# Attention and expert layer on one core: squarer transposes, scores two steps ahead, routing work on GpSimd

## The chip, the cores and the metric

The kernel runs on one core of a Trainium2 chip. The metric is the device time of one execution in microseconds. In the core, TensorE (PE in the profile) multiplies, VectorE (DVE), ScalarE (ACT) and GpSimd (POOL) do the rest, and SyncE (SP) issues transfers. Each engine works through its own instructions in the order in which they were written, and waits for the others by semaphores.

## The reference

Local and global causal attention over 4 batches, 8 heads, 768 positions and 64 columns a head, with a slope per head, and then a layer of 8 experts, of which each of the 3072 tokens takes two:

```python
keep = is_global | is_local             # 8 global positions; 96 local ones, the own included
scores = scale * q @ k.T + bias
scores = np.where(keep, scores, -1e9)
a = np.exp(scores - scores.max(-1))
a = a / (a.sum(-1) + 1e-09)
x = (a @ v)                             # then as [3072 tokens, 512]
noisy = x @ w_gate + np.log1p(np.exp(x @ w_noise)) * noise
top2 = two largest of noisy;  top2_w = softmax over the two
for e in range(8):                      # a token's rows for its two experts
    out[mask] += top2_w * (np.maximum(x[mask] @ w1[e], 0) @ w2[e])
```

## The kernel before

**Attention** goes over 24 blocks of 128 tokens (`g`), six to a batch, and in each over four pairs of heads (`hp`). One pass of the loop at the end of the attention part, an iteration, takes two pairs, `n` and `n + 1`; there are 48, and iteration k has n = 2k. A window is 168 keys wide: 96 earlier ones, 8 global ones, and 64 of the block's own, for each half of the 128 tokens. A batch's first block has only the 128 own ones.

- `score(n)` (L606): eight matmuls in the four corners of the array (64 x 64), into two banks of tag `sc`. VectorE adds the bias and takes the maximum (L628), ScalarE the exponential (L632). A pair's two windows lie in one of four standing buffers `a`, with 64 columns of zeros beside each; GpSimd writes the zeros once, at the start (L544).
- `trans(n)` (L635): four transposes a pair, 128 x 128 (L644), two in a first block, and ScalarE's copy (L646).
- `attend(n)` (L650): a pair's eight matmuls with the values (L666), each of 64 output rows; two of them, side by side in the two halves of the columns, run together. VectorE divides (L672 to L675).
- `gate_t`, `gate_l`, `gate_s` (L280 to L299): a block's gate and noise logits.

The order in an iteration is `trans(n)`, `trans(n+1)`, `score(n+2)`, `attend(n-2)`, `attend(n-1)`, and then what the table `todo` holds for these n (filled by `at`): loads, the gate, the splits of weights, the first tiles.

**Routing** is done in five segments of blocks (`SEG`, `route(r)`, L304): softplus as a polynomial in 13 steps (L321 to L336), the two largest (L342, L344), a token's place in its expert's list, and two marks and two entries a block (L408, L409), which TensorE multiplies into the lists (L417). `route` is a generator. `tick()` runs one step of each active segment, eight times an iteration; segments 0 and 1 take every other call. A step stands on VectorE in its place between the scores' reductions. Of a block's two marks one is on GpSimd and one on VectorE.

**Experts.** Each weight is split in two halves of 16 bits, by a scale from its maximum (`scales`, L143: four reductions of 1.2 us, L149). For expert 0 the first weight is split on GpSimd (`split`, L205, L206). After segment 2 (`CLOSE`), expert 0's first four tiles are gathered (L222), scaled and split (`ready`, `rest`, L233 to L250) and transposed (`turn_pe`, L264). Then the experts run: `up(e, c, f)` (L857) and `down`, and in between the rest of segments 3 and 4, the first of them in ten and then up to sixty calls around `up(0, 0, 0)` and `up(0, 0, 1)`. The first three `up` of expert 0 leave their subtraction to GpSimd (L865).

## Time and profile before

| | |
|---|---|
| median of 3 runs | 759.24 us (759.09 to 759.91) |
| the profiled execution | 757.7 us, of which the span 755.9 |
| TensorE busy in the span | 726.4 us, 96% |
| VectorE, ScalarE, GpSimd busy | 487.0, 359.3, 209.7 us |
| granted clock of TensorE, mean | 0.988 |
| iteration 0 of attention starts | 6.90 us |
| the first expert's first matmul | 192.38 us |

A busy share says which engine may be the bound of a stretch; it has to be read stage by stage, since attention and experts have different ones. A row of a timeline gives start, duration, engine, line and operation, output and inputs, shapes, and how many instructions it merges; in square brackets stands the idle time before it with what ended it. A matmul of 32 bits leaves two records. Matmuls overlap, so their spacing is read from the starts of rows.

### The profile page before, as it was taken

What the parts mean: (1) busy time and instruction counts of PE and PEld (TensorE: products, weight loads), DVE (VectorE), ACT (ScalarE), POOL (GpSimd) and SP (SyncE); (2) the same over time, 40 slices, a digit from 0 to 9 for tenths busy, and PEclk for the clock granted to TensorE, in tenths of its full rate; (3) what the DMA queues carried; (4) which work ended last, traced back from release to release, by engine and by line L of the source; (5) the groups of instructions that cost most, each with busy time, mean ns of one, the idle gap of its engine ahead of it and who ended that gap; (6) DMA issues with size and microseconds to landing.
All of it is one profiled execution on the core that took longest, in us unless ns stands there. A gap on an engine that the chain in (4) does not pass through costs nothing.

```text
span 755.9 us, 16638 instructions
## 1 busy us (share of the span) xinstructions
PE 726.4 (96%) x6279; PEld 454.3 (60%) x6279; DVE 487.0 (64%) x1655; ACT 359.3 (48%) x744; POOL 209.7 (28%) x209
## 2 busy tenths in 40 slices
PE   6999999897998999999999999999999999999996
PEld 4878867676544756464656556564656556564762
DVE  5657898878796747673865577276648646763500
ACT  5888787676344424333452434254344424342501
POOL 2000076230237451215031321403140322212014
PEclk9999999998899999999999999999999999999998
DMA  7889688964408865695479459546954864552015
GB/s 217 262 267 281 193 259 274 285 203 160 154 14 161 228 126 170 106 180 104 123 139 141 115 149 171 105 150 107 169 103 144 152 122 129 87 78 33 2 17 77
DMA packets 107673, 112.59 MB, mean 149 GB/s; under 512 B 53216, under 2 KB 66224, under 8 KB 107584
## 3 DMA queue, kind: packets, MB, share of 16 engines
q1 hardware_dynamic: 95104, 84.25, 41.0%
q0 software_dynamic: 11936, 26.92, 20.7%
q8 instruction: 52, 0.85, 0.5%
q14 instruction: 37, 0.30, 0.1%
q10 hardware_dynamic: 544, 0.26, 0.1%
HBM read 71.61 MB, written 28.10 MB: 132 GB/s over the span
## 4 chain that ended last, share of the span: by engine, by line
PE 72%; issue 12%; DVE 9%; POOL 3%; ACT 3%; DMA 1%; POOLq 0%; ACTq 0%; DVEq 0%
PE av L890 16%; PE at L857 15%; PE sc L857 14%; PE av L900 10%; PE at L644 5%; PE av L666 5%; PE sc L621 4%; POOL out_dram L875 2%; DVE ns L628 1%; PE sc L285 1%; DVE entry L409 1%; PE sc L293 1%; PE lg L299 1%; ACT a L632 1%; DVE l L238 1%
## 5 line engine op out<-in xcount | busy, mean ns | idle before, releaser
L875 POOL DMA_INDIRECT out_dram<-y,ids x56 | 88.6, 1583 | 211.7 <-ACT y L874 207.2
L857 PEld LDWEIGHTS <-w1h 128*128 128x128 f16 x1024 | 100.2, 99 | 70.7 <-issue 2.5
L857 PE MATMUL at<-xx,w1h 128*128 128x300 f16 (+1 forms) x512 | 128.7, 339 | 2.1 <-ACT xx L266 1.9
L857 PE MATMUL sc<-xx,w1h 128*128 128x300 f16 (+1 forms) x512 | 126.6, 336 | 0.0
L222 POOL DMA_INDIRECT xg<-xd,ids x56 | 57.4, 1026 | 166.5 <-DVE hl L868 124.2
L890 PE MATMUL av<-w2h,hh 128*128 128x512 f16 x256 | 97.1, 379 | 0.0
L890 PE MATMUL av<-w2l,hh 128*128 128x512 f16 x256 | 97.0, 379 | 0.0
L890 PE MATMUL av<-w2h,hl 128*128 128x512 f16 x256 | 97.0, 379 | 0.0
L857 PE MATMUL at<-xx,w1l 128*128 128x512 f16 (+1 forms) x256 | 86.7, 339 | 0.0
L857 PE MATMUL sc<-xx,w1l 128*128 128x512 f16 (+1 forms) x256 | 85.8, 335 | 0.0
L632 ACT ACTIVATE a<-ns,mx 128x168 f32<-128x168 f32 (+1 forms) x192 | 69.7, 421 | 32.7 <-DVE mx L628 28.4
L890 PEld LDWEIGHTS <-hh 128*128 128x128 f16 x512 | 49.5, 98 | 56.0
L868 DVE SCALAR_TENSOR_TENSOR hl<-sc,hh 128x300 f16<-128x300 f32 (+1 forms) x63 | 36.3, 577 | 67.4 <-ACT hh L867 67.4
L149 DVE TENSOR_REDUCE wmx<-raw 128x1 f32<-128x1024 f32 x64 | 76.5, 1207 | 0.0
L867 ACT ACTIVATE hh<-at 128x300 f16<-128x300 f32 (+1 forms) x62 | 31.2, 502 | 92.8 <-PE at L857 92.8
L900 PE MATMUL av<-hh,w2h 128*128 128x300 f16 x256 | 74.6, 291 | 0.0
L900 PE MATMUL av<-hh,w2l 128*128 128x300 f16 x256 | 74.3, 290 | 0.0
L900 PE MATMUL av<-hl,w2h 128*128 128x300 f16 x256 | 74.1, 290 | 0.0
L628 DVE CUSTOM_DVE_ANT_0 ns<-sc,bias 128x168 f32<-128x168 f32 (+1 forms) x192 | 53.8, 319 | 30.8 <-PE sc L621 19.7
L857 PEld LDWEIGHTS <-w1l 128*128 128x128 f16 x512 | 50.5, 99 | 38.4 <-issue 0.8
L868 DVE SCALAR_TENSOR_TENSOR hl<-at,hh 128x300 f16<-128x300 f32 (+1 forms) x62 | 35.5, 573 | 54.9 <-ACT hh L867 54.9
L242 ACT ACTIVATE xp<-xg,up 128x512 f16<-128x512 f32 x48 | 34.5, 719 | 71.6 <-DVE up L240 63.7
(174 smaller groups left out, 1215.1 us busy)
## 6 DMA issues: line engine op xcount, KB each, us to landing
raw<-in_w SPq DMA_DIRECT2D x32, 1024.0 KB, 7.8
out_dram<-zero SPq DMA_DIRECT2D x14, 512.0 KB, 6.9
vs<-in_v SPq DMA_DIRECT2D x24, 260.0 KB, 3.9
xd<-xr SPq DMA_DIRECT2D x24, 256.0 KB, 2.7
qs<-in_q SPq DMA_DIRECT2D x23, 256.0 KB, 5.9
ks<-in_k SPq DMA_DIRECT2D x19, 272.0 KB, 4.4
vp<-in_v SPq DMA_DIRECT2D x20, 195.0 KB, 5.3
ks<-in_k SPq DMA_DIRECT2D x4, 464.0 KB
```

What stands on the lines that cost most here:

```text
L149: nc.vector.tensor_reduce(m[:, i:i + 1], t[:, i % 2 * n:(i % 2 + 1) * n], op=OP.max, axis=AX.X, apply_absolute_value=True)
L222: nc.gpsimd.indirect_dma_start(out=xg[e, t], out_offset=None, in_=xd[:n], in_offset=bass.IndirectOffsetOnAxis(ap=rows(e, t), axis=0), boun ...
L242: nc.scalar.activation(y[:m, :Dm], x[:, :Dm], AF.Copy, scale=u)
L628: nc.vector.tensor_tensor_reduce(out=ns[:, s, :w], in0=ps[:, s], in1=bias[:, hp, s] if i else bias0[:, hp, s], scale=-scale, scalar=3e38, ...
L632: nc.scalar.activation(A[m][:, s, c:c + w], ns[:, s, :w], AF.Exp, bias=mx[:, s:s + 1], scale=-1.0)
L644: nc.tensor.transpose(p4[:, :, c, s * Q:(s + 1) * Q], x[:, s, a:a + P], ident)
L666: nc.tensor.matmul(ps[y * Q:(y + 1) * Q, h % 4], x[:kk, a:a + Q], t[:kk, c], start=kk < P or not i, stop=kk == P, tile_position=(0, y * Q))
L857: nc.tensor.matmul(ps, w[e % 2][:, k, fs], xx[c][:, x + k, :hh[c].shape[2]], start=n == 0, stop=n == 3 * KC - 1)
L868: nc.vector.scalar_tensor_tensor(hl[c][:, f], ps, 0.0, hh[c][:, f], op0=OP.max, op1=OP.subtract)
L875: ins = nc.gpsimd.indirect_dma_start(out=out, out_offset=bass.IndirectOffsetOnAxis(ap=rows(e, t), axis=0), in_=y, in_offset=None, bounds_c ...
L890: nc.tensor.matmul(ps, x[0][:, f, cols], w[e % 2][:, f], start=n == 0, stop=n == 3 * FC - 1)
L900: nc.tensor.matmul(ps, w[e % 2][:, f, cols], x[1][:, f], start=n == 0, stop=n == 3 * FC - 1)
```

## The change

- Standing buffers `a` go; a pair's two windows lie beside each other in 336 columns, in one of six rotating buffers. `trans` takes three squares of them, at columns 0, 208 and 104 (two squares in a first block), and ScalarE copies 384 columns instead of 512.
- `attend(n)` takes both pairs at once: 16 matmuls as before. Eight use the first two squares, on the two halves of the columns. Eight use the third: keys of one window in its rows 0 to 63, keys of the other in rows 64 to 103, so that they stand in two opposite corners of the array and write the two halves of one bank.
- The order in an iteration becomes `trans(n)`, `trans(n+1)`, `attend(n-2)`, `score(n+4)`. `score(0)` and `score(2)` come ahead of the loop, and the first half of the biases between them.
- In segments 0 to 3 the 13 polynomial steps go to GpSimd; it has no fused form, so they are 21 instructions. So do all marks of these segments. Segment 4 stays as it was.
- Expert 0's weights: loads, maxima and splits are some 18 to 36 pairs sooner.
- First tiles: four calls of `tick` between gathers instead of one; `ready` and `rest` of tile t at pairs 87 + 2t and 88 + 2t, and the transposes of the first three tiles inside the loop, at 90, 92 and 94.

```diff
+    def fused(eng, to, x, c, y, op0, op1, part):
+        if eng is nc.vector:
+            eng.scalar_tensor_tensor(to, x, c, y, op0=op0, op1=op1)
+        else:
+            eng.tensor_scalar(part, x, c, None, op0=op0)
+            eng.tensor_tensor(to, part, y, op=op1)
...
+        eng = nc.gpsimd if r + 1 < len(SEG) else nc.vector
...
-        nc.vector.tensor_mul(u, u, t)
+        eng.tensor_mul(u, u, t)
...
-            nc.vector.scalar_tensor_tensor(p, p, SP_C[j], t, op0=OP.add, op1=OP.mult)
+            fused(eng, p, p, SP_C[j], t, OP.add, OP.mult, p)
...
-                (nc.vector if j else nc.gpsimd).tensor_scalar(x, row, slf[:, 0, i, j:j + 1], None, op0=OP.is_equal)
+                (nc.vector if j and r + 1 == len(SEG) else nc.gpsimd).tensor_scalar(x, row, slf[:, 0, i, j:j + 1], None, op0=OP.is_equal)
...
                 gather(0, t, DUMP + z * P)
-                yield
+                for _ in range(4):
+                    yield
...
-            AW = WIN + Q
-            abuf = [ac.tile([P, 2, AW], F32, name=f"a{j}") for j in range(4)]
-            for t in abuf:
-                for x in range(2):
-                    nc.gpsimd.memset(t[:, x, (1 - x) * WIN:(1 - x) * WIN + Q], 0.0)
...
+            cols = (0, 2 * WIN - P, NP + NG) if i else (0, P)
+            w = len(cols) * P
+            ps = bank("at", 2)[:, :w]
             x = A.pop(n)
...
+            for j, a in enumerate(cols):
+                nc.tensor.transpose(ps[:, j * P:(j + 1) * P], x[:, a:a + P], ident)
+            AT[n] = aw.tile([P, 3 * P], F32, name="at", bufs=4)[:, :w]
...
+                if i:
+                    parts = (0, 0, vp[g], 0, NP + NG), (0, 1, vs[g], 0, P), (1, 0, vs[g], 0, Q), (1, 1, vp[g], Q, NP + NG)
+                else:
+                    parts = (0, 0, vs[g], 0, P), (0, 1, vs[g], 0, P)
...
+            run.sort(key=lambda x: x[:3])
...
+                nc.tensor.matmul(ps[y * Q:(y + 1) * Q, h % 4], w, t, start=id(x) in first, stop=id(x) in final,
+                                 tile_position=(r, y * Q))
...
-            for j in 22, 32, 50, 58, 76, 86:
+            for j in 6, 12, 18, 26, 50, 70:
                 at(j, load_w)
-            for x, places in (1, (34, 36, 42, 44, 46, 48)), (2, (58, 60, 66, 68, 70, 72)):
+            for x, places in (1, (16, 17, 20, 21, 23, 25)), (2, (28, 30, 34, 36, 38, 40)):
...
-                at(52 + 2 * j, split, 0, 1, j, nc.gpsimd)
+                at(27 + 3 * j, split, 0, 1, j, nc.gpsimd)
             for t in range(TA):
-                at(NPAIR - 5 + t, ready, 0, t)
-                at(NPAIR - 4 + min(t, 2), rest, 0, t)
+                at(NPAIR - 9 + 2 * t, ready, 0, t)
+                at(NPAIR - 8 + 2 * t, rest, 0, t)
+                if t < 3:
+                    at(NPAIR - 6 + 2 * t, lambda t: turn_pe(0, t, bank16("sc", 3)), t)
...
             score(0)
+            biases(bias, dist, range(HP))
+            score(2)
             for n in range(0, NPAIR + LAG, 2):
                 if n < NPAIR:
                     trans(n)
                     trans(n + 1)
-                if n + 2 < NPAIR:
-                    score(n + 2)
                 tick()
...
+                if n >= LAG:
+                    attend(n - LAG)
+                tick()
+                if n + 4 < NPAIR:
+                    score(n + 4)
+                tick()
```

What this does to the instructions' order is shown at three places. The first is TensorE in one iteration of the first batch: `at<-ident,a` are the transposes, `sc<-ks,qs` the scores, `av` the matmuls with the values, of the block before (`vp`) and of the block (`vs`). Before:

```order
L293 MATMUL sc<-xt,wgn 32x128 x4
L644 MATMUL at<-ident,a_197 128x2x64 x4
L644 MATMUL at<-ident,a_198 128x2x64 x4
L621 MATMUL sc<-ks,qs 64x168 x8
L666 MATMUL av<-vp_120,at 64x65 x2
L666 MATMUL av<-vs,at 64x65 x2
```

In the changed kernel:

```order
L285 MATMUL sc<-ident,xr 128x128 x4
L647 MATMUL at<-ident,a 128x128 x6
L674 MATMUL av<-vp_119,at 64x65
L674 MATMUL av<-vs,at 64x65
...
L626 MATMUL sc<-ks,qs 64x168 x8
L293 MATMUL sc<-xt,wgn 32x128 x4
```

Six transposes stand for eight, and the scores have moved behind the values. (`vp` and `vs` go on in turns for 16 matmuls in both.)

The second is GpSimd, from the last steps of segment 2's polynomial and marks to the first up-projection (`hl` is the subtraction of `up`, `mark` and `xd<-wd` belong to routing, `xg` is a gather, `ny` the polynomial's result). Before:

```order
L408 TENSOR_SCALAR mark<-row,slf_2891 128x128 x5
L370 DMA xd<-wd_3256 128x5x8
L408 TENSOR_SCALAR mark<-row,slf_3382 128x128 x5
L222 DMA xg<-xd,ids_85 128x520 x4
L370 DMA xd<-wd_3968 128x4x8
L408 TENSOR_SCALAR mark<-row,slf_4131 128x128 x4
L865 TENSOR_TENSOR hl_4125<-h,hh_4123 128x512 x3
```

In the changed kernel:

```order
L417 TENSOR_SCALAR mark<-row,slf_2964 128x128
L343 TENSOR_TENSOR p_3008<-p_3008,noise_s 128x40
L345 TENSOR_TENSOR ny_3009<-p_3008,l_3005 128x40
...
L222 DMA xg<-xd,ids_85 128x520 x4
...
L379 DMA xd<-wd_4078 128x4x8
L417 TENSOR_SCALAR mark<-row,slf_4167 128x128 x3
L873 TENSOR_TENSOR hl_4154<-h,hh_4152 128x512
L417 TENSOR_SCALAR mark<-row,slf_4167 128x128 x5
L873 TENSOR_TENSOR hl_4154<-h,hh_4152 128x512 x2
```

The polynomial's steps now stand between marks, and of segment 3's eight marks five stand behind the first up-projection's subtraction, where all four stood ahead of it.

The third is VectorE from expert 0's token list (`ids_85`) on; `l_79<-xg` is the first reading of a gathered tile, the `ISA` rows are the scores' reductions. Before, the reading comes four iterations later:

```order
L439 TENSOR_TENSOR ids_85<-find_3577,find_3578 128x4
L672 TENSOR_SCALAR den<-av 128x4
L673 RECIPROCAL den<-den 128x4
L675 TENSOR_TENSOR xr<-av,den 128x256
L628 ISA ns,mx<-sc,bias 128x168
...
L332 SCALAR_TENSOR_TENSOR p_3720<-l_3717,p_3720 128x32
L238 TENSOR_REDUCE l_79<-xg 128x1
```

In the changed kernel:

```order
L449 TENSOR_TENSOR ids_85<-find_3645,find_3646 128x4
L679 TENSOR_SCALAR den<-av 128x4
L680 RECIPROCAL den<-den 128x4
L682 TENSOR_TENSOR xr<-av,den 128x256
L633 ISA ns,mx<-sc,bias 128x168
...
L238 TENSOR_REDUCE l_79<-xg 128x1
```

Between list and reading there is now one iteration.

## Rows read from the trace of the kernel before

**Rows 1.** Busy time of each engine by stage; the first line names the columns.

```profile
core 0: us, PE busy (x) PEld busy (x) DVE busy (x) ACT busy (x) POOL busy (x), PEclk, DMA share, GB/s
20.74:82.75 62.01, 61.97 (x1160) 50.44 (x1158) 41.23 (x256) 52.27 (x135) 1.73 (x8) 1.00 0.84 266
82.75:163.37 80.62, 73.88 (x1289) 55.66 (x1285) 72.89 (x429) 61.45 (x156) 34.48 (x35) 1.00 0.79 249
163.37:192.38 29.01, 24.12 (x390) 19.44 (x387) 22.76 (x125) 18.70 (x43) 5.01 (x5) 0.88 0.48 165
192.38:242.87 50.49, 47.35 (x264) 22.62 (x265) 39.63 (x140) 22.21 (x39) 24.63 (x25) 0.97 0.41 107
242.87:755.90 513.03, 505.40 (x3015) 296.54 (x3014) 298.16 (x637) 193.12 (x345) 138.41 (x104) 0.99 0.60 120
```

**Rows 2.** Timeline of TensorE, from iteration 4 to iteration 6.

```profile
20.74 1.04 PE L644 MATMUL at<-ident,a 128*128 128x128 f32 x8
21.71 0.80 PE L621 MATMUL sc<-ks,qs 64*64 64x168 f32 x16
22.44 0.34 PE L666 MATMUL av<-vp,at 104*64 104x65 f32 x4
22.61 0.29 PE L666 MATMUL av<-vs,at 128*64 128x65 f32 x4
22.72 0.29 PE L666 MATMUL av<-vp,at 104*64 104x65 f32 x4
...
27.43 0.27 PE L644 MATMUL at<-ident,a 128*128 128x128 f32 x1
```

**Rows 3.** Waits up to 160 us: us in total, times, longest.

```profile
ACT a L632 <- POOL a L544: 3.1, 1, 3.1
```

**Rows 4.** Timelines of VectorE and TensorE in the first iterations.

```profile
5.17 0.29 DVE L628 CUSTOM_DVE_ANT_0 ns<-sc,bias 128x128 f32<-128x128 f32 x1
...
6.90 1.36 PE L644 MATMUL at<-ident,a 128*128 128x128 f32 x4 [1.79 <-ACT a L632]
```

**Rows 5.** VectorE's groups, 82.75 to 163.37 us: busy us, mean ns | idle before.

```profile
L149 DVE TENSOR_REDUCE wmx<-raw 128x1 f32<-128x1024 f32 x5 | 6.0, 1207 | 0.0
L408 DVE TENSOR_SCALAR mark<-row,slf 128x128 f16<-128x128 f16 x16 | 5.4, 340 | 0.0
...
L328 DVE SCALAR_TENSOR_TENSOR p<-p,t 128x40 f32<-128x40 f32 x12 | 2.3, 193 | 0.0
```

**Rows 6.** GpSimd's groups by shape, whole span.

```profile
L205 POOL TENSOR_SCALAR raw<-raw,wsc 128x512 f32<-128x512 f32 x12 | 19.8, 1648 | 12.9 <-ACT w1h L203 12.7
L408 POOL TENSOR_SCALAR mark<-row,slf 128x128 f16<-128x128 f16 x24 | 14.7, 621 | 24.4 <-DVE slf L401 15.0 <-DVE tab L420 5.2 <-DVE den L672 4.3
L206 POOL TENSOR_TENSOR w1l<-raw,w1h 128x512 f16<-128x512 f32 x12 | 14.0, 1166 | 1.0
...
L569 POOL IOTA iota_e<- 128x48 f32 x1 | 0.2, 216 | 0.0
```

**Rows 7.** The gathered tiles, 160 to 180 us: time from issue to landing.

```profile
DMA to landing us min/median/max: 5.3/6.7/7.1
```

**Rows 8.** Timeline of TensorE behind the last iteration of attention.

```profile
185.90 0.49 PE L666 MATMUL av<-vp,at 104*64 104x65 f32 x4 [3.24 <-ACT at L646]
```

**Rows 9.** Timelines of TensorE and GpSimd around the first up-projection, and five marks.

```profile
155.80 2.97 POOL L408 TENSOR_SCALAR mark<-row,slf 128x128 f16<-128x128 f16 x5 [5.19 <-DVE tab L420]
...
197.27 0.38 PE L857 MATMUL at<-xx,w1l 128*128 128x512 f16 x1
...
199.07 1.15 POOL L865 TENSOR_TENSOR hl<-h,hh 128x512 f16<-128x512 f32 x1 [2.96 <-ACT hh L864]
...
242.87 0.82 PE L857 MATMUL at<-xx,w1h 128*128 128x300 f16 x2 [1.94 <-ACT xx L266]
```

**Rows 10.** TensorE's groups, 20.74 to 82.75 us.

```profile
L666 PE MATMUL av<-vs,at 128*64 128x65 f32 x304 | 18.1, 221 | 0.0
```

More of the change, by code (lines that the diff above doesn't have):

```diff
@@ L636, in trans @@
             g, hp, b, i = geo(n)
-            w = 2 * P if i else P
-            ps = bank("at", 2)[:, :2 * w]
-            p4 = ps.rearrange("p (x c t) -> p x c t", x=2, t=P)
+            cols = (0, 2 * WIN - P, NP + NG) if i else (0, P)
+            w = len(cols) * P
+            ps = bank("at", 2)[:, :w]
             x = A.pop(n)
-            for s in range(2):
-                for c in range(w // P):
-                    a = AW - P if c + 1 == w // P else 0
-                    nc.tensor.transpose(p4[:, :, c, s * Q:(s + 1) * Q], x[:, s, a:a + P], ident)
@@ new lines, in attend @@
+            run, first, final = [], set(), set()
+            for m in n, n + 1:
+                g, hp, b, i = geo(m)
+                x = AT.pop(m)
+                if hp % 2 == 0:
+                    ps = bank("av", 2)[:, :4 * D1].rearrange("p (h d) -> p h d", h=4)
+                if i:
+                    parts = (0, 0, vp[g], 0, NP + NG), (0, 1, vs[g], 0, P), (1, 0, vs[g], 0, Q), (1, 1, vp[g], Q, NP + NG)
+                else:
+                    parts = (0, 0, vs[g], 0, P), (0, 1, vs[g], 0, P)
+                for k, y, t, r, e in parts:
+                    for z in range(2):
+                        a = (2 * k or y) * P + z * Q
+                        h = 2 * hp + z
+                        run.append((k, h, y, x[r:e, a:a + Q], t[r:e, h * D1:(h + 1) * D1], r))
@@ new lines, in attend @@
+            run.sort(key=lambda x: x[:3])
+            for y in range(2):
+                mine = [x for x in run if x[2] == y]
+                first.add(id(mine[0])), final.add(id(mine[-1]))
+            for x in run:
+                k, h, y, w, t, r = x
+                nc.tensor.matmul(ps[y * Q:(y + 1) * Q, h % 4], w, t, start=id(x) in first, stop=id(x) in final,
+                                 tile_position=(r, y * Q))
+            if hp == 1:
+                XR[g] = gp.tile([P, H, D], F32, name="xr", bufs=2)
@@ L678, in tile_local_global_attention_then_moe @@
+            den = aw.tile([P, 4], F32, name="den", bufs=2)
+            nc.vector.tensor_scalar(den, ps[:, :, D], 1e-9, None, op0=OP.add)
+            nc.vector.reciprocal(den, den)
+            h0 = 2 * hp - 2
+            nc.vector.tensor_mul(XR[g][:, h0:h0 + 4], ps[:, :, :D],
+                                 den[:, :, None].to_broadcast([P, 4, D]))
         todo = {}
```

60 lines of the change are left out of this document (12 added, 48 removed).

## The prediction

> **What bounds the kernel now.** I read the stages first [rows 1]. From 242.87 us to the end TensorE is busy 505.4 of 513.0 us, and the change issues nothing there but the same experts' matmuls: that part stays. Before it lie 192.4 us of attention and routing and 50.5 us of the first expert's entry, and all that the change touches is in these 243 us. From 20.74 to 82.75 us TensorE is busy 61.97 of 62.01 us, VectorE only 41.2: this stretch is TensorE's. From 82.75 to 163.37 us VectorE is busy 72.9 of 80.6 us, and its 20 iterations (two head pairs each) take 4.03 us in the mean, against 3.26 for the 19 before: this one is VectorE's. From 163.37 to 192.38 us, where attention ends and the first expert's tiles are made, no engine is full, and the granted clock falls to 0.88.
>
> One iteration of the first stretch [rows 2]: eight transposes in 0.97 us (20.74 to 21.71), that is 0.121 us each; eight score matmuls in 0.73 us; then 32 records of attention-times-values, four of them (two matmuls, one on each half of the columns) every 0.117 us, 0.029 us a record. Two iterations take 27.43 - 20.74 = 6.69 us, 3.345 each, because the gate's matmuls alternate.
>
> The sum is made against the profiled execution (755.9 us span, 757.7 in all); the median of the runs is 759.24, 1.5 more, and I subtract the same savings from it.
>
> **The start (iterations 0 to 3).** ScalarE's first exponential waits 3.1 us for GpSimd to zero the buffers of the weights [rows 3]. These buffers are gone; the maximum it then needs is there by 5.46 us (the first reduction starts at 5.17 and takes 0.29), while the transposes behind it start at 6.90 [rows 4]: I take 0.9 us of these 1.4. The second gain is the order: scores now run two steps ahead, so a transpose no longer waits for the exponentials of the score just made. From 6.90 to 20.74 four iterations took 13.84 us, though their work on TensorE is some 2 x 3.15 + 2 x 2.5 = 11.3 after the change (both worked out below). So 0.9 + 2.5, I take 3.5 us, between 1 (only the buffers) and 5.
>
> **The squares (iterations 4 to 22).** Of the 19, two belong to a batch's first block, which keeps two transposes a pair. In the other 17, two of eight transposes go: 0.243 us. The value matmuls stay 16, but a half of them now reads a third square, in which rows 0 to 63 hold one half's keys and rows 64 to 103 the other's; these run on opposite corners of the array. No row shows such a pair. The nearest are the 32 records above at 0.029 us, and the scores, which use all four corners and have 16 records in 0.73 us, 0.046 us each with longer rows. So the third square costs between nothing more and 16 x (0.046 - 0.029) = 0.27 us. I take 0.05, the step by which the first four records behind the scores are slower (0.17 against 0.117), for one more change of tile shape, and else the value rows' price, whose size and operands these have. 17 x (0.243 - 0.05) = 3.3 us saved; bounds 4.1 saved (no cost) and 0.5 lost (0.27). ScalarE copies a quarter less, which was hidden.
>
> The Trainium skill has a rule against this: TensorEngine Tiling (Array Packing), Restrictions and Gotchas, says that different row tiles cannot access the same PSUM bank simultaneously, and the two corners write one bank. If that made them take turns, eight matmuls of 0.117 us would follow one another where four slots stood: +0.47 us an iteration, the second rival below. In this case's trace the scores' row tiles write two banks, so it doesn't decide.
>
> **VectorE's stretch (iterations 23 to 42, 80.6 us).** What leaves VectorE here [rows 5]: 16 marks, 5.4 us; expert 0's five remaining maxima, 6.0 us, and some 1.2 us of short steps behind them, which now run in iterations 8 to 21 (there VectorE has 20 us to spare); the polynomials of two segments, 12 steps of 0.193 and 14 others like them, 5.1 us. Sum 17.7 of 72.9, leaving 55.2. TensorE then needs 16 x 3.15 (3.345 - 0.243 + 0.05) + 4 x 2.5 (first blocks: four transposes and 16 value records fewer than now) = 60.4 us and becomes the bound on the mean. The leftover isn't even: the order puts entries, list steps and one segment's end on the same five iterations, where VectorE's rows add up to 3.4 to 4.9 us; I add 5 us. One new wait comes on top. GpSimd must do 21 instructions for a segment's polynomial, and in segment 2 they queue among the last marks of segment 1, six of them ahead of the polynomial's end (second order excerpt). A mark takes 0.62 us there [rows 6]; the small operations have no row of their own: between 0.22 (an iota of 48 columns) and 0.38 (the mark's 0.62 less 88 columns, at the 2.7 ns a column that lie between it and the scaling of 512 columns, 1.65). I take 0.33, nearer to the upper end, because they read two operands as the marks' kind does. 6.9 + 3.7 = 10.6 us, while VectorE comes to the maxima after 14 of its slots, eight to an iteration: 5.7. So it would wait 4.9 us (2.6 at the lower price), with the next scores' reductions queued behind it, and TensorE's transposes behind those. Scores two steps ahead leave TensorE 2.1 us of other work (transposes 0.73, values 0.94, gate 0.4); 2.8 are left. GpSimd's load in this stretch hardly grows otherwise: eight splits of 2.8 us leave it for iterations 13 to 24, 16 marks and 42 small operations come, 0.3 us more for collisions. 60.4 + 5 + 2.8 + 0.3 = 68.5, so 12.1 saved; bounds 18 (TensorE alone, and 2 us of waits) and 5 (three segments with such a wait, none absorbed).
>
> **Making the first tiles (iteration 43 to the first expert's matmul, 29.0 us).** In the changed order there is one iteration between the token list and the first tile's reading, four before. A gather lands 6.7 us after its issue [rows 7]; an iteration is 3.1, so VectorE waits 3.6 us at that reading (third order excerpt), and the next reductions queue behind it. After that it has 22.8 - 2.5 (segment 3's polynomial gone) = 20.3 us of work to the end of the stage, and hand-overs with ScalarE, 3.1 us of today's 6.2 idle: 27.0, so 2.0 saved. Bounds: 7.5 saved (TensorE alone: five iterations of 3.15 and some 6 us of tail) and 1 lost. What it does remove is the 3.24 us wait of TensorE at 185.90, after which the clock fell to its lower level, 1.2 GHz: the granted clock of the two stages, 0.12 short over 29.0 us and 0.03 short over 50.5 us, adds up to 3.5 + 1.5 = 5.0 us lost [rows 1, 8], 1.5 of them behind 192.38.
>
> **The first expert's entry: a new wait.** Attention's last iterations make four calls fewer of segment 3's routing, so only three of its eight marks are issued before the first up-projection; the other five stand behind GpSimd's subtraction of that up-projection's result (second order excerpt), and TensorE's list matmuls, which need all eight, stand ahead of the second up-projection. Now the last matmul of the first one ends at 197.65, GpSimd's subtraction at 200.22, and five marks took 2.97 us [rows 9]: TensorE waits 2.57 + 2.97 = 5.5 us. It waited 3.24 us at 185.90, and the clock fell; here I expect the same, 4.6 us of the 5.0, where now 1.5 are lost. The wait at 242.87 (1.94 us) may shrink behind a later TensorE; I take 0.6 of it off. 5.5 + 4.6 - 1.5 - 0.6 = 8.0 lost. Bounds: 3.5 (the clock stays) and 10.
>
> **Sum:** -3.5 - 3.3 - 12.1 - 2.0 + 8.0 = -12.9 us; 759.24 - 12.9 = 746.3.
>
> **Rivals.** (1) The wait behind the marks isn't there, since segment 3 gets further or TensorE is late anyway: 738.3. For it: its length hangs on three marks out of eight. Against: the order is fixed. (2) The opposite corners take turns: +0.47 us in 17 iterations is 8.0; in VectorE's stretch TensorE would need 67.9 instead of 60.4, and half of that comes on top of the peaks: 4 more. 758.3, no change. (3) GpSimd becomes the bound of routing: no wait at the maxima is absorbed, 12.1 shrinks to 5: 753. (4) The slower side: records of the third square don't run together at all. One lasts 0.22 us from start to end [rows 10], 16 in a row 3.5 us instead of 0.47, +3.0 in some 38 iterations: 860. It decides from 0.56 us more an iteration, when the savings of 12.9 are eaten (17 x 0.56 + 16 x 0.06 + what the first blocks and the start lose, about 2.4), that is from 0.064 us a record against 0.029. Against all of (2) and (4): the scores' four corners overlap well.
>
> **Chances.** The forecast with its bounds 0.68; (1) 0.10; (2) 0.09; (3) 0.08; (4) 0.05. The range reaches from rival (1) with a little more from the bounds of VectorE's stretch, 737, to just under (2), 757. Within 0.2% is what a measurement of this kernel can't tell from no change (757.7 to 760.8). Faster: forecast, (1), (3), without the bad ends: 0.84. Same: most of (2): 0.07. Slower: (4) and the rest of (2): 0.09.
>
> **What would show it.** Iterations of 3.1 to 3.2 us up to segment 1 and value records 0.029 us apart in the third square; VectorE's idle time before the maxima of segment 2, released by GpSimd; idle time before the first tile's reading, released by a gather; TensorE idle some 5.5 us after the first up-projection, released by GpSimd's mark, and the lower clock behind it. Wrong would be: iterations still of 3.35 us (the corners), no idle time at that mark (rival 1), or a change behind 242.87 us.

## The result and the profile after

The changed kernel takes 768.25 us (median of 4 runs, 767.4 to 770.3) against 759.16 before: a ratio of 1.0139, 95% interval 1.0110 to 1.0168. It is slower by some 9 to 10 us, where the prediction said 13 us faster. Its profiled execution takes 767.7 us, the span 766.0, which is 10.1 more than before. (Runs that took far longer than the others of their kernel, one of e10's and two of the kernel before's, are left out of medians and ratios.)

Busy time of each engine in the changed kernel, by the stages of [rows 1]: iterations 0 to 3, 4 to 22, 23 to 42, the first tiles, the first expert's entry, the rest.

```profile
core 0: us, PE busy (x) PEld busy (x) DVE busy (x) ACT busy (x) POOL busy (x), PEclk, DMA share, GB/s
6.87:19.56 12.69, 11.39 (x155) 8.49 (x154) 9.49 (x57) 8.07 (x24) 0.00 (x0) 1.00 0.78 214
19.56:90.70 71.14, 63.03 (x1133) 50.42 (x1131) 48.26 (x261) 50.41 (x140) 22.75 (x40) 0.95 0.83 263
90.70:171.61 80.91, 70.65 (x1252) 55.95 (x1248) 57.94 (x371) 53.50 (x150) 40.92 (x83) 0.92 0.75 235
171.61:197.55 25.94, 19.97 (x365) 15.81 (x361) 19.02 (x102) 16.01 (x42) 10.88 (x26) 1.00 0.42 134
197.55:252.59 55.04, 48.93 (x266) 22.92 (x265) 39.15 (x143) 22.55 (x39) 27.80 (x30) 0.94 0.42 106
252.59:766.00 513.41, 505.37 (x3015) 296.50 (x3014) 298.10 (x637) 193.15 (x345) 138.10 (x104) 0.99 0.59 120
```

| stage | before, us | after, us | forecast of the difference | measured |
|---|---|---|---|---|
| iterations 0 to 3 | 13.84 | 12.69 | -3.5 | -1.2 |
| iterations 4 to 22 | 62.01 | 71.14 | -3.3 | +9.1 |
| iterations 23 to 42 | 80.62 | 80.91 | -12.1 | +0.3 |
| 43 to the first expert's matmul | 29.01 | 25.94 | -2.0 | -3.1 |
| entry, to its second half | 50.49 | 55.04 | +8.0 | +4.6 |
| the rest | 513.03 | 513.41 | 0 | +0.4 |

TensorE does less work in the second stage than its 71 us: it is idle for 8 us, where before it was never idle [rows 1]. VectorE is no longer near full in the third (57.9 of 80.9 us, before 72.9 of 80.6), as was meant, and the stage is no shorter. So waits took the place of work. The lower clock is a part of it: what the stages' granted clocks miss of 1.00, times their lengths, adds up to 13.3 us from 19.56 to 252.59, where the same sum before is 5.0 [rows 1]. How much of that cost time is not known, since TensorE also waits in these stretches. Iteration by iteration (start to start, us):

| iterations | 4 to 9 | 10 to 12 | 13 to 18 | 19 to 22 | of these, 21 | 39 |
|---|---|---|---|---|---|---|
| before | 20.07 | 9.21 | 19.36 | 13.37 | 3.55 | 5.77 |
| after | 18.73 | 14.69 | 18.02 | 19.70 | 8.18 | 11.82 |

Undisturbed iterations save 0.22 us each (forecast 0.19). Three places cost most. The first is iteration 10. Timeline of VectorE there, in the changed kernel (start, duration, engine, operation; in brackets the idle time before and what ended it):

```profile
41.27 0.43 DVE L682 TENSOR_TENSOR xr<-av,den 128x256 f32<-128x256 f32 x1 [2.71 <-DMA xd<-xr]
```

Timeline of SyncE's queue, some nine microseconds earlier:

```profile
32.56 0.48 SPq L140 DMA_DIRECT2D raw<-in_w  x1
33.15 0.79 SPq L282 DMA_DIRECT2D xd<-xr  x1
```

Timeline of TensorE:

```profile
42.30 1.20 PE L626 MATMUL sc<-ks,qs 64*64 64x128 f32 x16 [1.96 <-issue]
```

VectorE's division writes a block's result into one of two buffers (`xr`), and waits until the store of an earlier block has left it. That store was issued at 33.15, right behind the load of 1 MB of weights, and lets go at 41.27. (The result itself was complete at 29.2; SyncE issued its store 3.9 us later, behind other loads. In e8, a version below without the early weights, that is 3.3 us.) The reductions stand behind the division, and the scores behind the reductions.

The second and third places are iterations 21 and 39, where VectorE waits for GpSimd's polynomial. Such waits of the whole span (us in total, times, longest):

```profile
DVE m L351 <- POOL ny L345: 13.3, 3, 6.4
```

Timeline of VectorE in iteration 21:

```profile
83.87 0.17 DVE L351 MAX8 m<-ny 128x8 f32<-128x8 f32 x1 [5.51 <-POOL ny L345]
```

GpSimd ahead of it:

```profile
80.16 0.29 POOL L310 TENSOR_TENSOR p<-t,p 128x48 f32<-128x48 f32 x1
80.42 1.57 POOL L205 TENSOR_SCALAR raw<-raw,wsc 128x512 f32<-128x512 f32 x1
82.08 1.15 POOL L206 TENSOR_TENSOR w1l<-raw,w1h 128x512 f16<-128x512 f32 x1
83.19 0.29 POOL L343 TENSOR_TENSOR p<-p,noise_s 128x48 f32<-128x48 f32 x1
83.55 0.29 POOL L345 TENSOR_TENSOR ny<-p,l 128x48 f32<-128x48 f32 x1
```

VectorE in iteration 39:

```profile
152.61 0.17 DVE L351 MAX8 m<-ny 128x8 f32<-128x8 f32 x1 [6.43 <-POOL ny L345]
```

GpSimd ahead of it:

```profile
150.50 0.27 POOL L310 TENSOR_TENSOR p<-p,u 128x40 f32<-128x40 f32 x1
150.74 0.31 POOL L309 TENSOR_SCALAR t<-l 128x40 f32<-128x40 f32 x1
151.13 0.27 POOL L310 TENSOR_TENSOR p<-t,p 128x40 f32<-128x40 f32 x1
151.38 0.61 POOL L417 TENSOR_SCALAR mark<-row,slf 128x128 f16<-128x128 f16 x1
151.96 0.27 POOL L343 TENSOR_TENSOR p<-p,noise_s 128x40 f32<-128x40 f32 x1
152.31 0.27 POOL L345 TENSOR_TENSOR ny<-p,l 128x40 f32<-128x40 f32 x1
```

Both times VectorE's first maximum waits for the last step of GpSimd's polynomial: at 21 a split of weights stands two steps from its end, at 39 marks stand between its steps. (The third of these waits, 1.4 us, is segment 1's, in iteration 31.) Small steps that depend on each other start 0.36 to 0.42 us apart there, where the prediction took 0.33. Last, the entry. Timeline of TensorE:

```profile
201.92 0.20 PE L426 MATMUL lg<-entry,mark 128*128 128x64 f16 x1 [0.41 <-POOL mark L417]
204.50 0.20 PE L426 MATMUL lg<-entry,mark 128*128 128x64 f16 x1 [2.38 <-POOL mark L417]
...
206.82 0.24 PE L426 MATMUL lg<-entry,mark 128*128 128x64 f16 x1 [0.34 <-POOL mark L417]
```

Timeline of GpSimd:

```profile
202.71 1.15 POOL L873 TENSOR_TENSOR hl<-h,hh 128x512 f16<-128x512 f32 x1 [0.85 <-ACT hh L872]
203.84 2.92 POOL L417 TENSOR_SCALAR mark<-row,slf 128x128 f16<-128x128 f16 x5
```

This is the wait that was forecast: five marks behind the subtraction, and 5.7 us from the first list matmul (201.17) to the second up-projection (206.87), where 5.5 were expected.

### The profile page after: what moved, and what is told of

It is laid out like the page before. It is cut to its first block, busy times and chain, and to the rows that moved or that the text cites. A ratio compares the mean times of both kernels' runs of the same rounds, so it can differ in the third digit from the quotient of the medians.

```text
span 766.0 us, 16326 instructions
## 1 busy us (share of the span) xinstructions
PE 721.9 (94%) x6199; PEld 451.9 (59%) x6199; DVE 475.8 (62%) x1583; ACT 346.5 (45%) x744; POOL 245.2 (32%) x305
## 4 chain that ended last, share of the span: by engine, by line
PE 69%; issue 12%; POOL 8%; DVE 5%; ACT 3%; DMA 3%; SPq 0%; POOLq 0%; ACTq 0%; DVEq 0%
PE av L898 16%; PE sc L865 15%; PE at L865 15%; PE av L908 10%; PE av L674 3%; PE at L647 3%; PE sc L626 2%; POOL out_dram L883 2%; POOL mark L417 2%; DMA xd<-xr 1%; PE sc L285 1%; DVE ns L633 1%; POOL p L309 1%; POOL p L310 1%; DMA qs<-in_q 1%
## 5 line engine op out<-in xcount | busy, mean ns | idle before, releaser
L865 PE MATMUL sc<-xx,w1h 128*128 128x300 f16 (+1 forms) x512 | 128.4, 340 | 0.0
L222 POOL DMA_INDIRECT xg<-xd,ids x56 | 57.9, 1035 | 163.6 <-DVE hl L876 123.8
L898 PEld LDWEIGHTS <-hh 128*128 128x128 f16 x512 | 49.4, 98 | 56.1
L626 PE MATMUL sc<-ks,qs 64*64 64x168 f32 (+1 forms) x768 | 46.7, 328 | 17.8 <-DVE m L351 9.1
```

Of the source, the lines that this page charges most:

```text
L222: nc.gpsimd.indirect_dma_start(out=xg[e, t], out_offset=None, in_=xd[:n], in_offset=bass.IndirectOffsetOnAxis(ap=rows(e, t), axis=0), boun ...
L626: nc.tensor.matmul(ps[y * Q:(y + 1) * Q, s], qq[r, 2 * i0 + s, c], kk[r, c, k0:k0 + w], start=True, stop=True, tile_position=(hp % 2 * D, ...
L865: nc.tensor.matmul(ps, w[e % 2][:, k, fs], xx[c][:, x + k, :hh[c].shape[2]], start=n == 0, stop=n == 3 * KC - 1)
L898: nc.tensor.matmul(ps, x[0][:, f, cols], w[e % 2][:, f], start=n == 0, stop=n == 3 * FC - 1)
```

## The experiments

The changed kernel is the base unless another is named. Stages and iterations are from one profiled execution each; the same code in iterations 23 to 42 took 76.6, 77.1 and 79.3 us in three kernels below, at granted clocks of 1.00, 1.00 and 0.94, so differences of 2 or 3 us there say little. Ratios are to the kernel before on the same chip. Its median there was 756.6 us for e1 to e4, 762.2 for e5 to e8, 761.0 for e9 to e11, 762.4 for e12 and 758.6 for e13 to e15; the expectations were written in microseconds, but totals of different groups compare by the ratio.

| kernel | median, us | ratio (95%) | 4 to 22 | 10 to 12 | 23 to 42 | tiles | entry |
|---|---|---|---|---|---|---|---|
| before | | 1 | 62.0 | 9.2 | 80.6 | 29.0 | 50.5 |
| after | 768.3 | 1.0139 (1.0110 to 1.0168) | 71.1 | 14.7 | 80.9 | 25.9 | 55.0 |
| e1 polynomials on VectorE | 757.1 | 0.9997 (0.9972 to 1.0021) | 68.0 | 13.2 | 73.7 | 26.3 | 55.1 |
| e2 weights as before | 773.6 | 1.0216 (1.0177 to 1.0256) | 57.3 | 8.7 | 96.9 | 29.8 | 56.9 |
| e3 marks shared | 767.4 | 1.0113 (1.0049 to 1.0176) | 71.0 | 13.2 | 77.0 | 29.5 | 56.1 |
| e4 all three undone | 754.6 | 0.9969 (0.9946 to 0.9993) | 57.7 | 8.7 | 80.0 | 29.8 | 52.6 |
| e5 four calls | 767.6 | 1.0091 (1.0062 to 1.0120) | 70.5 | 14.1 | 81.0 | 29.6 | 52.4 |
| e6 e4, one step ahead | 763.0 | 1.0010 (0.9973 to 1.0047) | 61.5 | 9.2 | 85.7 | 33.4 | 49.0 |
| e7 e4, tiles as before | 756.1 | 0.9927 (0.9896 to 0.9959) | 57.4 | 8.9 | 83.9 | 32.2 | 53.7 |
| e8 mixed | 749.4 | 0.9846 (0.9790 to 0.9901) | 57.5 | 8.9 | 77.1 | 30.9 | 50.4 |
| e9 before, order alone | 759.0 | 0.9980 (0.9959 to 1.0001) | 61.1 | 9.1 | 76.6 | 33.2 | 55.8 |
| e10 e8, weights between | 753.7 | 0.9931 (0.9896 to 0.9965) | 62.4 | 9.2 | 77.3 | 30.4 | 49.0 |
| e11 e8, early loads | 754.1 | 0.9914 (0.9888 to 0.9940) | 62.0 | 13.3 | 76.6 | 30.6 | 51.7 |
| e12 e11, three results | 750.5 | 0.9855 (0.9777 to 0.9933) | 58.2 | 9.7 | 79.3 | 30.5 | 50.8 |
| e13 after, three results | 767.9 | 1.0114 (1.0079 to 1.0149) | 69.6 | 11.8 | 80.7 | 30.0 | 57.0 |
| e14 e13, marks on VectorE | 758.9 | 0.9991 (0.9969 to 1.0012) | 68.5 | 11.3 | 77.8 | 29.1 | 50.3 |
| e15 e12, early maxima | 752.1 | 0.9920 (0.9895 to 0.9945) | 65.8 | 11.8 | 74.8 | 29.8 | 49.2 |

### What stands in whose way: the four suspects

**e1.**

```diff
-        eng = nc.gpsimd if r + 1 < len(SEG) else nc.vector
+        eng = nc.vector
```

> The changed kernel with the polynomial steps of all segments back on VectorE; nothing else differs. Theory (VectorE's maxima wait for GpSimd's polynomial, 5.5 us behind the splits in iteration 21 and 6.4 us between the marks in iteration 39, and TensorE stands behind that): iteration 21 falls from 8.18 to about 3.5 us and iteration 39 from 11.82 to about 4, VectorE gets some 5 us of work back in a stretch where it has room; 756 to 760 us. Rival (VectorE was the bound there and is so again, the waits only showed where it stood): those iterations shrink, but their neighbours grow by as much; 766 to 768 us.

757.1 us; iteration 21 takes 3.32 us, 39 takes 5.35. The theory holds: beside the early weights and the marks, the polynomials on GpSimd cost some 11 us. The rival has a small part: iterations 19 and 20 take 5.57 and 5.94 us, where before and after had 3.1 to 3.9, with VectorE busy 12.2 of the 15 us from 69 on and the granted clock at 0.89.

**e2.**

```diff
-            for j in 6, 12, 18, 26, 50, 70:
+            for j in 22, 32, 50, 58, 76, 86:
...
-                at(27 + 3 * j, split, 0, 1, j, nc.gpsimd)
+                at(52 + 2 * j, split, 0, 1, j, nc.gpsimd)
```

> The changed kernel with the loads, maxima and splits of expert 0's weights at the pairs where the kernel before had them. Theory (the four loads between 21 and 55 us fill the DMA engines, whose share of 20 to 40 us is 1.04, and queries and keys come late): iterations 10 to 12 fall from 6.01, 5.01 and 3.67 us to 3.1, 3.4 and 2.65, 5.5 us less; of that some comes back where the maxima and splits now fall among the marks and polynomials; 762 to 766 us. Rival (attention has become faster and runs up against its own queries and keys, whatever the weights do): iterations 10 to 12 stay above 4 us; 767 to 770 us.

Iterations 10 to 12 take 8.7 us, so the weights are to blame for the stall. The total was a miss, 773.6: the splits now stand among segment 1's polynomial and marks, and iteration 31 takes 19.33 us. VectorE there:

```profile
116.31 0.17 DVE L351 MAX8 m<-ny 128x8 f32<-128x8 f32 x1 [12.92 <-POOL ny L345]
```

**e3.**

```diff
-(nc.vector if j and r + 1 == len(SEG) else nc.gpsimd).tensor_scalar(
+(nc.vector if j else nc.gpsimd).tensor_scalar(
```

> The changed kernel with every second mark back on VectorE in all segments. Theory (TensorE's 5.7 us between the first and the second up-projection are five marks behind GpSimd's subtraction): the idle time there goes, the stretch from the first expert's first matmul to its second half's first falls from 55.0 to about 50.5 us; segment 2's polynomial has three or four marks of 0.7 us fewer ahead of it, 2 us off iteration 39; 760 to 763 us. Rival (the list matmuls wait for entries and routing anyway, marks were only the last named): the stretch stays above 53 us; 766 to 768 us.

A miss: the entry takes 56.1 us and the total is 767.4. Of GpSimd's four marks two still stand behind the subtraction, and TensorE waits 3.05 us for the first of them; the granted clock from 194 to 216 us is 0.67. Iteration 39 is 1.8 us shorter, as expected. Half the marks are not half the wait.

**e4.** The three edits above together.

> The changed kernel with all three undone: polynomials on VectorE, marks shared, weights at the old pairs. What is left of the change are the three squares, the scores two steps ahead and the first tiles made one by one. Theory (these are sound, the three others cost): 0.23 us an iteration in iterations 4 to 22 (4.4), the start 1.2, the first tiles 3, nothing in VectorE's stretch; 749 to 752 us, faster than before. Rival (the order with scores two steps ahead is what starves VectorE and TensorE of each other, the three only show it): 756 us or more.

754.6 us, faster than before by 0.1 to 0.5%. That is some 2 us on this chip (756.6 before), where 7 to 10 were expected: on the total a miss. Iterations 4 to 22 are 4.3 us shorter, 23 to 42 unchanged, the first tiles and the entry together 2.8 us longer. So the squares, the order and the tiles do no harm together, and the rest of the change costs all of the loss; each of the three by itself this does not show.

### Why the early weights cost

**e11.** From the mixed version e8 (below), only the loads early:

```diff
-            for j in 22, 32, 50, 58, 76, 86:
+            for j in 6, 12, 18, 26, 76, 86:
```

> The mixed version with the first four loads as early as in the changed kernel (pairs 6, 12, 18, 26), but maxima and splits at the old pairs. Theory (the loads alone make queries and keys late): iterations 10 to 12 take 12 to 14.5 us together instead of 8.9; 753 to 756 us. Rival (the maxima, 1.2 us of VectorE each in iterations 8 to 12, do it): they stay below 9.5 us; 748 to 750 us.

Iterations 10 to 12 take 13.3 us: the loads alone do it. **e12** gives the results a third buffer:

```diff
-                XR[g] = gp.tile([P, H, D], F32, name="xr", bufs=2)
+                XR[g] = gp.tile([P, H, D], F32, name="xr", bufs=3)
```

> The mixed version with the first four loads early, as in the run before it, and three buffers for a block's result (xr) instead of two. Theory (the early load stands ahead of the result's store in SyncE's queue and takes its bandwidth; VectorE's division waits 3.8 us for that store, and the reductions behind it keep the scores back): the wait for the store goes, iterations 10 and 11 fall from 6.17 and 4.49 us to about 3.5 and 3.3, 4 us less; 749 to 751 us. Rival (the scores wait for the next batch's queries, which land late for the same reason, and VectorE's wait only runs beside that): iteration 10 stays above 5 us, with TensorE idle before the scores; 753 to 755 us.

9.7 us and 750.5: the theory holds. The waits of e11 from 37 to 50 us (us in total, times, longest):

```profile
DVE xr L682 <- DMA xd<-xr: 3.8, 1, 3.8
```

Busy time by window in e11 (columns as above):

```profile
20.00:40.00 20.00, 19.10 (x378) 15.52 (x374) 10.31 (x66) 13.37 (x38) 1.73 (x8) 1.00 1.06 357
40.00:60.00 20.00, 18.53 (x311) 14.60 (x313) 12.05 (x75) 15.32 (x46) 0.00 (x0) 0.91 0.98 305
```

The same windows in e12:

```profile
20.00:40.00 20.00, 19.55 (x387) 15.86 (x386) 12.26 (x78) 16.32 (x46) 1.73 (x8) 1.00 1.06 355
40.00:60.00 20.00, 20.00 (x384) 16.00 (x385) 12.43 (x79) 15.55 (x47) 0.00 (x0) 1.00 1.06 337
```

The DMA engines are as full as with the stall (share 1.06, then 1.06 where it was 0.98), yet TensorE is busy 39.6 of the 40 us. The full DMA engines cost at most the 0.8 us that iterations 10 to 12 still take over e8's 8.9; the two buffers cost the rest. On the total the two ratios' intervals overlap.

**e13** is the same edit on the changed kernel.

> The changed kernel with three buffers for a block's result instead of two; nothing else differs. Theory (its stall in iterations 10 to 12 is VectorE waiting for the store of a block's result behind the early loads): iterations 10 to 12 fall from 14.7 to about 10 us together, everything behind moves up; 762 to 765 us. Rival (in the changed kernel the maxima of the weights in iterations 8 to 12 hold VectorE up as well, and fill the gap): they stay above 12.5 us; 766 to 768 us.

Iterations 10 to 12 fall from 14.7 to 11.8 us, between the two expectations: the store is 2.9 us of the stall. (The same code took 13.2 to 14.7 us there in the changed kernel, e1, e3 and e5, and 11.8 and 11.3 in e13 and e14, so this is 1.3 to 3.4 us.) Most of the rest are the maxima: e15 (below) differs from e12 in their place alone, and takes 11.8 us where e12 takes 9.7. The total stays at 767.9: in the profiled execution tiles and entry take 87.0 us instead of 81.0, at granted clocks of 0.86 and 0.89 where they were 1.00 and 0.94, with the same instructions in both. Why the clock was lower was not found.

### What the polynomial costs on GpSimd

**e14.** From e13, all marks of segments 0 to 3 on VectorE:

```diff
-(nc.vector if j and r + 1 == len(SEG) else nc.gpsimd).tensor_scalar(
+(nc.vector if j or r + 1 < len(SEG) else nc.gpsimd).tensor_scalar(
```

> The changed kernel with three buffers for a block's result, and all marks of segments 0 to 3 on VectorE, so that segment 2's polynomial is alone on GpSimd. Theory (VectorE's maxima wait for GpSimd because the polynomial queues behind marks of 0.7 us; alone, its 21 instructions take 8.0 us from the first to the last against some 5.7 us of VectorE's own work): the wait in iteration 39 falls from 6.4 to about 2 us and the iteration from 11.8 to 6 or 7 us; iterations before it are longer by the marks, 3 to 5 us; 758 to 763 us. Rival (GpSimd is too slow for these small steps whatever else it does): iteration 39 stays above 9 us; 764 to 767 us.

Segment 2's polynomial alone takes 7.8 us (139.98 to 147.75) instead of 10.8 (141.75 to 152.58) and VectorE waits 2.4 us instead of 6.4; iteration 39 takes 8.29 us instead of 11.82. The waits of e14, 140 to 160 us:

```profile
DVE m L351 <- POOL ny L345: 2.4, 1, 2.4
```

So 4.0 of the 6.4 us went with the marks, which VectorE now does itself, and 2.4 are the steps' own. (Each step that is one instruction on VectorE is written as two for GpSimd, L309 and L310 in the rows above; whether GpSimd could do it in one no run tries.) The entry's wait behind GpSimd's marks is gone too (50.3 us), and the total is that of the kernel before.

### The entry

**e5.** Routing's four missing calls put back:

```diff
+                elif n + 4 == NPAIR:
+                    for _ in range(4):
+                        tick()
```

> The changed kernel with four more calls of the routing's steps in the last iteration but one, those that its two-steps-ahead order leaves out. Theory (segment 3's marks stand behind GpSimd's subtraction only because routing got four calls less far): all eight marks are done before the first up-projection's result, TensorE's 5.7 us of idle time at the list matmuls go and the granted clock with them stays; the stretch from the first expert's first matmul to its second half falls from 55.0 to about 50.5 us; 763 to 765 us. Rival (VectorE has these steps to do anyway, and doing them sooner delays the first tiles by as much): that stretch shrinks, the one before it grows; 767 to 769 us.

By the stages the rival holds: the entry falls by 2.6 us, the tiles before it grow by 3.6. The total doesn't decide: by the ratio it is some 3.6 us below the changed kernel's, but the intervals overlap. And the theory's condition came about only in part: seven of the eight marks stand ahead of GpSimd's subtraction, one behind, and the second up-projection still starts 3.9 us after the first list matmul (203.44 to 207.38), where it was 5.7.

### Squares, order and tiles

**e6.** From e4, the scores one step ahead:

```diff
+                if n + 2 < NPAIR:
+                    score(n + 2)
                 tick()
...
-                if n + 4 < NPAIR:
-                    score(n + 4)
...
-            score(2)
```

> The kernel with polynomials, marks and weights undone, and the scores again one step ahead, between the transposes and the values. What stays are the squares and the first tiles. Theory (the order matters where VectorE or ScalarE is late, at the start and at VectorE's peaks, the squares everywhere): iterations 4 to 22 stay at 57.7 us, the start takes 1.5 us more, iterations 23 to 42 grow by 2 to 4 us from 80.0; 757 to 760 us. Rival (the squares alone do it, two steps ahead give nothing): 754 to 755 us, with every stretch as it is with two steps.

A surprise: 61.5 us in iterations 4 to 22, not 57.7. The squares alone save 0.06 us an iteration. **e9** is the other half, on the kernel before: `score(n + 4)` behind the values, six standing buffers, the biases ahead of the loop, no squares.

```diff
-                if n + 2 < NPAIR:
-                    score(n + 2)
...
...
+                if n + 4 < NPAIR:
+                    score(n + 4)
...
```

> The kernel before with its scores two steps ahead and behind the values, and nothing else: eight transposes an iteration from standing buffers (six now), no third square. Theory (what the order gives in iterations 4 to 22 is one change of the array's tile shape saved, because the third square's matmuls and the scores both use 64-row tiles; without the third square there is nothing to save): two iterations stay near 6.69 us, the stretch at 61 to 62 us; the waits behind the exponentials go at the start and in iterations 23 to 42, 2 to 4 us; 755 to 758 us. Rival (the order by itself is worth 0.16 us an iteration): two iterations take 6.35 us, the stretch 59 us; 751 to 753 us.

Two iterations still take 6.69 us: the order alone saves nothing there. The two need each other: together, in e4, they save 0.23 us an iteration. Timeline of TensorE in iteration 4 of e6:

```profile
20.62 0.80 PE L626 MATMUL sc<-ks,qs 64*64 64x168 f32 x16
21.35 0.27 PE L674 MATMUL av<-vp,at 104*64 104x65 f32 x1
...
21.98 0.27 PE L674 MATMUL av<-vp,at 40*64 40x65 f32 x1
22.08 0.22 PE L674 MATMUL av<-vs,at 64*64 64x65 f32 x1
...
22.58 0.43 PE L293 MATMUL sc<-xt,wgn 128*32 128x128 f32 x8
```

And in iteration 4 of e4:

```profile
19.50 0.27 PE L674 MATMUL av<-vp,at 104*64 104x65 f32 x1
...
20.13 0.27 PE L674 MATMUL av<-vp,at 40*64 40x65 f32 x1
20.23 0.22 PE L674 MATMUL av<-vs,at 64*64 64x65 f32 x1
...
20.52 0.35 PE L626 MATMUL sc<-ks,qs 64*64 64x168 f32 x1
...
20.59 0.22 PE L674 MATMUL av<-vp,at 40*64 40x65 f32 x1
20.64 0.74 PE L626 MATMUL sc<-ks,qs 64*64 64x168 f32 x14
21.30 0.43 PE L293 MATMUL sc<-xt,wgn 128*32 128x128 f32 x8
```

In e6 values take 1.23 us (21.35 to 22.58) where before took 1.08 (from 22.44 [rows 2] to the gate's matmul at 23.52): one more change of shape, 0.15, against 0.22 for two transposes saved. In e4 the third square's records stand next to the scores, which use 64-row corners as well. The scores begin at 20.52 among the last of them, and both together take 1.17 us (20.13 to 21.30) instead of 0.60 + 0.73 = 1.33 in e6. The Trainium skill (TensorEngine Tiling (Array Packing), Key Properties) says that changing the tiling mode drains TensorE while changing the tile does not; these rows agree, with 0.15 us for the additional change. That the shape is the cause is read from the rows, not tried by itself.

In iterations 23 to 42 the order seems to help on its own: 76.6 us in e9 against 80.6, and e4 against e6 80.0 to 85.7 (granted clocks 0.96 and 0.92). In e9 it was given back in tiles and entry, 89.0 us at clocks of 0.77 and 0.89.

**e7.** From e4, the tiles as before:

```diff
-                at(NPAIR - 9 + 2 * t, ready, 0, t)
-                at(NPAIR - 8 + 2 * t, rest, 0, t)
+                at(NPAIR - 5 + t, ready, 0, t)
+                at(NPAIR - 4 + min(t, 2), rest, 0, t)
...
```

> The kernel with polynomials, marks and weights undone, and the first tiles gathered, read and transposed at the places of the kernel before. Theory (VectorE's 4.2 us of waiting for the first gathered tile, which hold up the reductions behind it, are traded for a longer end): iteration 44 falls from 7.09 to about 3.5 us, but the transposes of all four tiles then stand at the end; from iteration 43 to the first expert's matmul it is 29 to 30 us again, 754 to 756 us. Rival (the wait is pure loss): that stretch falls to 26 us, 751 us.

Inconclusive: the stage takes 32.2 us at a granted clock of 0.84 against 29.8 at 0.94, and the two ratios' intervals overlap. The wait itself is there in e4, 4.17 us of VectorE for the first gathered tile, and gone in e7; iteration 44 is no shorter (6.72 against 7.09).

### A version faster than both

**e8.** Polynomials on VectorE, weights as before, four calls, and:

```diff
-(nc.vector if j and r + 1 == len(SEG) else nc.gpsimd).tensor_scalar(
+(nc.vector if j and r + 2 >= len(SEG) else nc.gpsimd).tensor_scalar(
```

> The kernel with polynomials on VectorE and weights at the old pairs, the marks of segments 0 to 2 on GpSimd, those of the last two shared, and four more calls of the routing's steps in the last iteration but one. Theory (of the change's moves to GpSimd only the marks are free, since nothing on VectorE waits for them): iterations 23 to 42 fall from 80.0 to 76 or 77 us, the 3.2 us of waiting behind the marks at the first expert's entry go; 747 to 751 us. Rival (VectorE's time is not what limits iterations 23 to 42, or the list matmuls then wait for GpSimd): that stretch stays at 80 us; 753 to 755 us.

749.4 us, a ratio of 0.985 (0.979 to 0.990): faster than both (the changed kernel has 1.014). The entry takes 50.4 us, without the wait; iterations 23 to 42 take 77.1. **e10** and **e15** try to take the maxima out of these as well, e10 from e8 with

```diff
+            for j in 18, 26, 32, 40, 58, 76:
...
+            for x, places in (1, (28, 29, 30, 31, 33, 35)), (2, (43, 45, 47, 49, 51, 53)):
```

> The mixed version (polynomials on VectorE, marks of the first three segments on GpSimd, four more calls) with expert 0's loads at pairs 18, 26, 32 and 40 and all its maxima at pairs 28 to 53, the splits at the old pairs. Theory (loads and maxima are worth moving, only not into the first 50 us): iterations 10 to 12 stay at 8.9 us together, iterations 23 to 42 fall from 77 to about 73 us, since five maxima of 1.2 us leave VectorE there; 744 to 747 us. Rival (the loads are late for nobody only where they were, or the maxima now meet segment 0's polynomial): iterations 4 to 22 grow from 57.5 by as much; 749 to 752 us.

and e15 from e12 with

```diff
+            for x, places in (1, (16, 17, 22, 23, 25, 27)), (2, (30, 31, 36, 37, 39, 41)):
```

> The mixed version with early loads and three buffers for a block's result, and expert 0's maxima at pairs 16 to 41. Theory (VectorE has room for them there, and five of 1.2 us leave its full stretch): iterations 23 to 42 fall from 79 to 73 or 74 us, iterations 4 to 22 stay within 1 us of 58.2; 745 to 748 us. Rival (VectorE's room in iterations 14 to 20 goes to segment 0's polynomial, which is on VectorE here): iterations 14 to 22 grow by 4 us or more; 749 to 751 us.

e10: the rival, and more: 753.7 us. Iterations 16 and 17 take 5.56 and 5.19 us, 25 and 26 take 5.07 and 4.71. e15: 23 to 42 falls to 74.8, as the theory says, and 4 to 22 grows to 65.8, as the rival says: iterations 19 and 20, with segment 0's polynomial, take 5.40 and 5.32. Both totals lie above even the rivals' ranges. VectorE's spare time there, 20 us on the sum, is not free in the iterations that matter. Busy time in iterations 23 to 42 of e15 (columns as above):

```profile
84.43:159.26 74.83, 67.92 (x1252) 53.54 (x1248) 61.92 (x397) 57.06 (x157) 43.52 (x51) 0.98 0.78 241
```

## Why the prediction failed, point by point

The span grew by 10.1 us, where the sum said 12.9 less. Of these 23 us two terms account for 24.8, and the others give 1.8 back: iterations 4 to 22 (forecast -3.3, measured +9.1), where the early weights were put at nothing, and iterations 23 to 42 (forecast -12.1, measured +0.3), where the bound on the mean was too low and the wait for GpSimd too short.

- **Start.** -1.2 instead of -3.5; -2.0 in e4. The step that failed is adding two gains of which one uses up the other. The 0.9 us from the zeroed buffers are there, since ScalarE's first exponential starts at 5.51 us instead of 6.45. But iteration 0 starts at 6.87, before at 6.90, because the matmuls of `score(2)` now stand ahead of it; in e6, without `score(2)` there, it starts at 6.08. Of the 2.5 us for the order 1.2 came: iterations 0 and 1 take 3.67 and 3.44 us, where the sum has 2.5 each (1.1 us of the first is a wait for queries that e4, with the same code there, does not have).
- **Squares.** Two undisturbed iterations take 6.24 us (38.29 less 19.56, by three), 0.22 less each, forecast 0.19. That the size came out is luck: the third square's change of shape costs 0.15, not 0.05, and the order, to which I gave nothing here, gives 0.16. The opposite corners run together (0.029 us a record): rival (2) and the rule of the Trainium skill that the prediction cites, on one PSUM bank, show no cost here.
- **What was missing from the sum.** The step that failed in iterations 4 to 22: I moved the loads, maxima and splits of expert 0 there (by 16 to 32 pairs, as the diff has it) and put them at nothing. Iterations 10 to 12 grew by 5.5 us; the loads cost 4.5 by themselves (e11 against e8), through a store and a buffer that the change does not touch. Iterations 19 to 22 grew by 6.3; a split stands in segment 0's polynomial, and VectorE waits 5.5 us in iteration 21. I saw VectorE's 20 spare us and the early splits in GpSimd's queue, and counted only segment 2's wait.
- **VectorE's stretch.** The wait at segment 2's maxima was seen, 6.4 us instead of 4.9 (steps 0.37 us apart instead of 0.33, and marks). That 2.1 of it would be absorbed was wrong: iteration 39 grew by 6.0 us, and the clock of the stage fell to 0.92. The bound on the mean was wrong as well, and e15 shows it without that wait: VectorE has 11 us less to do there than before (61.9 for 72.9), and the stage is only 5.8 us shorter. TensorE's term of 60.4 us was mis-sized: it is busy 67.9 us. Of the difference 4.1 us are routing's own matmuls (L384 to L388 and L426), which lie in this stretch and not in the one from which 3.15 us an iteration was taken. Beyond that, I had added 5 us for unevenness; what is left here is 6.9.
- **First tiles.** -3.1, forecast -2.0; the wait for the gather is there, 0.9 us in the changed kernel and 4.2 in e4 (forecast 3.6). But this stage took 25.9 to 33.4 us in these kernels, at clocks from 1.00 to 0.77, so the agreement proves little.
- **Entry.** The mechanism and its 5.7 us (forecast 5.5) were right. The stage lost 4.6, not 8.0. TensorE's idle time in it grew by 3.0 us only (55.0 less 48.9 against 50.5 less 47.4), since segment 4's list matmuls, which waited before three times for 0.38 us, now wait for nothing, and its busy time by 1.6, where I had put 4.6 less 1.5 for the clock; the granted clock was 0.94. The wait at the stage's end stayed (1.91 us), where I took off 0.6. Rival (1) is out.
- **Range and rivals.** Rival (3) was the nearest in its mechanism, GpSimd as the bound of routing, with 753. Its price of one unabsorbed wait left out the splits, and no rival put the weights' transfers against attention's own.

## What to carry to other kernels

Before handing work to an idle engine, list what already stands in its queue where the result is needed: 21 small steps of 0.37 us were bearable by themselves (a wait of 2.4 us) and dear among marks (6.4) or splits and marks (12.9). A large transfer that is moved forward has to be priced by what queues behind it, small stores above all, and by how many buffers wait for them: one more buffer took 3.7 us off iterations 10 to 12 in e12. Time freed on an engine counts only in the iterations where that engine is late, not on the sum over a stretch. And the engine that becomes the bound has to be summed with all its work in that stretch, routing's matmuls included.

## What the runs showed of the hardware

- A store of 256 KB, issued 0.6 us behind a load of 1 MB in SyncE's queue, held its buffer for 8.1 us (33.15 to 41.27), where the median of these stores on the profile's page is 2.9 from issue to landing. The Trainium skill (DMA: Bandwidth & Descriptors, Queues, rings and completion order) says that each DMA engine consumes a queue's descriptors in ring order, while a later one may still finish first. The row fits the first half, and shows no more than that the store was late.
- With DMA engines at a share of 1.06 TensorE was busy 39.6 of 40 us (e12), once VectorE no longer waited for one particular store.
- Small steps on GpSimd (128x40, fp32) take mostly 0.27 us (tensor_tensor) and 0.31 to 0.35 us (tensor_scalar); 21 of them in a chain took 7.8 us with nothing between them (e14), where a fused step on VectorE takes 0.19 us [rows 5].
- What reads as one more change of the array's tile shape in an iteration cost 0.15 us (1.23 us for the values in e6, 1.08 before); where the third square and the scores, both on 64-row tiles, are neighbours, the two together take 0.16 us less (1.17 for 1.33).
- Tiles and entry, with nearly the same instructions, took 79 to 89 us in the seventeen kernels, longer at a lower granted clock: 78.9 us at 0.94 and 1.00, 89.0 at 0.77 and 0.89. The four whose entry had 0.89 took 85.6 to 89.0, the others 78.9 to 85.9. What decides that clock stays open.
